# The second mixture's first steps taken batch by batch, with batch 0's operands made during the first mixture

## The chip, the cores and the metric

The kernel runs on one core of a Trainium2 chip: TensorE (PE, matrix products), VectorE (DVE), ScalarE (ACT), GpSimd (POOL) and SyncE (SP, which here only issues loads and stores). The metric is the device time of one execution in microseconds; less is better. A profiled execution gives a trace of every engine.

## The reference, cut to what matters

An attention with a local and a global window makes x (2 batches of 768 rows, 512 columns), then come two mixtures. The second is a layer norm, a product up to 2048 features, a relu, a product down, and a sum with its input:

```python
def _moe_ref(x, mu_k, mu_r, w_k, w_v, w_r):
    x_prev = np.concatenate([np.zeros((B, 1, D)), x[:, :-1, :]], axis=1)
    xk = mu_k * x + (1.0 - mu_k) * x_prev
    xr = mu_r * x + (1.0 - mu_r) * x_prev
    k = np.maximum(xk @ w_k, 0.0)
    v = k * k @ w_v
    r = 1.0 / (1.0 + np.exp(-(xr @ w_r)))
    return r * v

def _moe2_ref(x, g_ln, w_ch1, w_ch2):
    mu = np.mean(x, axis=-1, keepdims=True)
    var = np.mean((x - mu) ** 2, axis=-1, keepdims=True)
    xn = (x - mu) / np.sqrt(var + 1e-06) * g_ln
    ch = np.maximum(xn @ w_ch1, 0.0) @ w_ch2
    return x + ch
```

## The kernel before

Every operand of a product is split into a high and a low part, and a product of two operands is three products: high by high, low by high, high by low. A high part is a rounded copy (ScalarE); a low part is the operand less its high part (VectorE or GpSimd).

The first mixture works on six groups of 256 rows, `g` = 0 to 5; groups 0 to 2 are batch 0, 3 to 5 batch 1. For each group `plan_k` makes xk (`plan_mix`) and the product with `w_k` (L745), squares the relu (L754, L755) and splits it (L756, L760); `plan_r` does the gate (L709, tanh in L714); `plan_v` does the product with `w_v` (L786 to L788, three matmuls of 512 columns for each of 8 feature chunks and 2 row blocks) and, with the gate, writes x1 (L800). x1 of a group stays on the chip to the end and takes up the result.

The second mixture takes each batch of 768 rows as two halves of 384, interleaved by blocks of 128 rows, and does the product up by a scheme of seven products in place of eight (P1 to P7 in `plan_up`, L1029, six matmuls of 384 columns each), so it needs sums of blocks of the normalised rows and sums of blocks of the weights. `plan_norm(s, i, ...)` prepares block `i` of batch `s`: statistics (L819, L820, VectorE), root (L823, L824, GpSimd), normalised block `ln` (L832, VectorE), four transposes on TensorE into bank 7 (L828, called a turn here), copies (ScalarE), and, in line 834, sums and low parts. Of each two blocks, the even one gives the parts `b0h`/`b0l` (batch 0) or `b1h`/`yy` (batch 1), the odd one `b0r` or `m`/`u`, and both together eight sums in `h` that are split into `t0h`/`t0l` or `t1h`/`t1l`.

A step is one pair of feature chunks (`q` = 0 to 7, 256 features by the scheme's two halves) for one batch `s`. Before, step `k` is `q, s = divmod(k, 2)`: batch 0 and batch 1 in turn. `plan_up(k)` makes the seven products, adds them up out of the banks (L1037, VectorE), applies the relu and the high part (ScalarE) and the low part `h` (L1048). `plan_down(k)` multiplies with `w_ch2` (L1122 to L1124) and adds to x1 (L1128, L1138). `plan_w1` and `plan_w2` load and convert the weights of a pair (64-bit words: L590 or L588, L592 to L595), scale them (L973), make the four sums (L982 to L985) and split (L601, L605). The pair's first weights lie in `s0` or `s1`, by the parity of `q`.

The order is set by a planner, `Plan`: each operation names engines with an assumed duration, the cells it reads and writes, the rooms (buffers) it needs and a due time. `play` always takes the operation that can start first by the planner's own clock, and among equals the one due first. So an engine's order follows from these numbers; on the chip each engine then executes its instructions in that order. `self.mixed` and `self.free` are operations behind which others must stand: the last product of `plan_k` for the last group, and the last x1 of group 1.

Of the kernel before, what the change touches and what calls it, by code (L numbers as in the profile page):

```python
# [8 lines left out]
F32 = mybir.dt.float32  # L9
F32R = mybir.dt.float32r  # L10
# [6 lines left out]
P = 128  # L17
# [197 lines left out]
class Fast:  # L215
# [467 lines left out]

    def plan_r(self, g, due):

        nc, p = self.nc, self.plan
        if g < EG:
            z = Part([self.H0, self.token("xr", 1)], lambda t, _: t[:, 0:2].rearrange("p a b n -> p a (b n)"))
        else:
            z = self.room("t0h", 1, [P, 2, 1024], F32R)  # L690
        rooms = [z]
        put = lambda: tuple(z.tile[:, i].rearrange("p (c t) -> p c t", c=4) for i in range(2))
        self.plan_mix(g, 1, rooms, put, "xr", due)
        if g < 2:
            if g == 0:
                self.e01 = self.room("b0r", 1, [P, 4, 512])
            e = [(self.e01, lambda tb=tb: self.e01.tile[:, 2 * g + tb, :]) for tb in range(2)]
        else:
            zs = [self.room("g" if g % 2 else "e", 2, [P, 512]) for _ in range(2)]
            e = [(z, lambda z=z: z.tile) for z in zs]  # L700
        self.e[g] = e
# [62 lines left out]
    def plan_v(self, g, due):  # L764
# [7 lines left out]
        def make():  # L772
            x = self.x1[g] = self.t([P, 4 * (GT + 1)], "xg", bufs=6)
            return x

        x1 = Room("xg", 6, make, True)
        parts = [(tb, f, f + 4) for tb in range(2) for f in (0, 4)]
# [26 lines left out]
    def plan_norm(self, s, i, due, low_due):  # L804
# [8 lines left out]
        up = [self.mixed, self.x_op] if late else [self.mixed]  # L813
        o = slice(j * P, (j + 1) * P)
# [15 lines left out]
        p.op({"DVE": 850}, stats, [("x1", g, tb)], [N], [st], due, behind=[self.free])  # L830
        p.op({"POOL": 400}, root, [], [N], [st], due)
        p.op({"DVE": 550}, lambda e: nc.vector.tensor_scalar(y.tile, x(), st.tile[:, 6:7], st.tile[:, 0:1], ALU.subtract, ALU.mult), [], [N], [st, y], due + 1)  # L832
        p.op({"PE": 436}, turn, [], [N], [y, b], due + 2)
        sub = lambda e, z, u, v: (nc.vector if e == "DVE" else nc.gpsimd).tensor_tensor(z, u, v, ALU.subtract)
        if i % 2 == 0:
            hi, lo = (lambda z=z: z.tile[:, 0 : 4 * TS].rearrange("p (c t) -> p c t", c=4)[:, :, o] for z in X[0:2])
            p.op({"ACT": 590}, lambda e: self.copy(e, F(), b.tile), [N], [("F", j)], [b, prep], due + 3)
            p.op({"ACT": 590}, lambda e: self.copy(e, hi(), chunks(b.tile)), [N], [("B", s, i, 0)], [b, X[0]], due + 3)
            p.op({"POOL": 1440}, lambda e: sub(e, lo(), chunks(F()), hi().bitcast(F32)), [("F", j), ("B", s, i, 0)], [("B", s, i, 1)], [prep, *X[0:2]], low_due, behind=up)
            return  # L840
# [14 lines left out]
        else:  # L855
            p.op({"ACT": 400}, lambda e: self.copy(e, hi(), pair(y.tile[:, 256:512])), [N], [("B", s, i, 0)], [y, X[2]], due + 3)
            p.op({"POOL": 700}, lambda e: sub(e, lo(), pair(y.tile[:, 256:512]), hi().bitcast(F32)), [N, ("B", s, i, 0)], [("B", s, i, 1)], [y, *X[2:4]], due + 4)
        p.op({"DVE": 350} if s and i == 5 else {"POOL": 700}, lambda e: sub(e, T(2), T(1), F()[:, 0:256]), [Tt[1], ("F", j)], [Tt[2]], [prep], due + 4)
        p.op({"DVE": 350} if s and i == 5 else {"POOL": 700}, lambda e: sub(e, T(3), F()[:, 256:512], T(1)), [Tt[1], ("F", j)], [Tt[3]], [prep], due + 4)
        eight = lambda: prep.tile[:, 1536:2560].rearrange("p (k t) -> p k t", k=8)  # L860
        p.op({"ACT": 1050}, lambda e: self.copy(e, th(), eight()), Tt, [("T", s, i, 0)], [prep, X[4]], due + 5)
        p.op({"DVE": 1250} if s else {"POOL": 2500}, lambda e: sub(e, tl(), eight(), th().bitcast(F32)), [*Tt, ("T", s, i, 0)], [("T", s, i, 1)], [prep, *X[4:6]], due + 5)

    def first(self, last):
# [12 lines left out]
        with self.tc.manual_schedule(engines=ORDERED):  # L877
# [29 lines left out]
            self.plan_k(1, at[1], at[1] - 8)  # L907
            self.plan_v(0, at[1] + 12)
            for g in range(1, NG):
# [7 lines left out]
                if EG <= g + 1 < NG:  # L917
                    self.plan_r(g + 1, at[g + 1] - 12)
# [4 lines left out]
    def plan_second(self, start):  # L923
# [39 lines left out]
    def plan_w1(self, q, c, due, behind=()):  # L963
# [35 lines left out]
    def plan_up(self, k, due):  # L999

        nc, p = self.nc, self.plan
        q, s = divmod(k, 2)
# [6 lines left out]
        u3, order = 21, self.ORDER  # L1009
# [78 lines left out]
    FIRST = {"P1": -6.0, "P6": -5.7, "P7": -5.4, "P2": 0.0, "P4": 1.1, "P5": 2.2, "P3": 3.3}  # L1088
    ORDER = {"P1": 0.0, "P6": 1.1, "P5": 5.0, "P7": 6.1, "P2": 10.0, "P4": 11.1, "P3": 15.0}

    def plan_down(self, k, due):

        nc, p = self.nc, self.plan
        q, s = divmod(k, 2)
# [4 lines left out]
        for m in range(3):  # L1099
# [5 lines left out]
            elif k == 0 and m == 1:  # L1105
                rooms = [self.bank_room(i) for i in (3, 6)]
# [5 lines left out]
            d = due + (3 * m if lone else 2.2 + 4.9 * m if k else m - 6)  # L1112
# [256 lines left out]
```

## Time and profile before

| | |
|---|---|
| three runs, median (lowest to highest) | 563.97 us (563.05 to 565.64) |
| the profiled execution | 562.92 us |
| its span, first to last instruction | 561.1 us |
| mean granted clock of TensorE | 0.984 of full speed |
| TensorE matmuls busy | 528.3 us, 94% of the span |
| VectorE busy | 403.2 us, 72% |
| GpSimd busy | 305.0 us, 54% |
| ScalarE busy | 288.4 us, 51% |

Busy time is the time in which an engine has an instruction at work; the granted clock says how fast TensorE could run then. Matmuls overlap, so the distance from one start to the next is the price of one, not its own duration. A row of the timeline gives the start, the duration, the engine, the line, the tiles, and in brackets how long the engine stood idle before and what ended that. Batch 0's first turn is at 244.96 us, the last product of the first mixture ends at about 296.6 us, and the second mixture's first product is at 281.94 us.

### The profile page before, as it was taken

Reading aid. Unit: us, or ns where it says so; the run is one execution under the profiler, and the core shown is the slowest. Engines: PE = TensorE matmul, PEld = TensorE weight load, DVE = VectorE, ACT = ScalarE, POOL = GpSimd, SP = SyncE. Lnnn points to the kernel's source line nnn. Section 1 sums busy time; section 2 is a strip of 40 time slices with the busy share of each in tenths; the row PEclk is TensorE's granted clock in tenths of the full one; section 3 lists DMA queues with packets and bytes.
Section 4 is the critical chain, followed back from the end, with each engine's and each line's share of the span. In section 5 each row is a group of like instructions: output and inputs, shape, how many; then the busy total and the mean of one; then the engine's idle time right before and its main releaser. Section 6 shows DMA issues by size and latency. Waiting matters only on the chain.

```text
span 561.1 us, 8802 instructions
## 1 busy us (share of the span) xinstructions
PE 528.3 (94%) x3178; PEld 455.9 (81%) x3178; DVE 403.2 (72%) x766; ACT 288.4 (51%) x639; POOL 305.0 (54%) x365
## 2 busy tenths in 40 slices
PE   5879899999999999999797899999999999999995
PEld 4657677878799888888686798888998889888983
DVE  4987998776787535346979888767697767868463
ACT  2878877768453213245535365464555536464320
POOL 3266775565633121109777579586495738686200
PEclk9999999999999999999979899999999999999998
DMA  8899765512210000001210131313031311311024
GB/s 167 193 226 204 190 187 131 136 39 77 76 39 1 2 1 0 1 1 37 77 37 1 37 114 37 113 38 114 0 114 38 91 61 39 114 37 39 0 77 155
DMA packets 59456, 42.64 MB, mean 76 GB/s; under 512 B 49036, under 2 KB 49292, under 8 KB 59404
## 3 DMA queue, kind: packets, MB, share of 16 engines
q1 hardware_dynamic: 58796, 41.33, 28.1%
q8 instruction: 27, 0.44, 0.3%
q10 hardware_dynamic: 576, 0.66, 0.3%
q14 instruction: 25, 0.20, 0.1%
q0 software_dynamic: 32, 0.00, 0.0%
HBM read 38.84 MB, written 3.15 MB: 75 GB/s over the span
## 4 chain that ended last, share of the span: by engine, by line


## 5 line engine op out<-in xcount | busy, mean ns | idle before, releaser
L1128 DVE TENSOR_TENSOR xg<-b,xg 128x1024 f32<-128x1024 f32 x44 | 53.7, 1221 | 36.9 <-PE b L1124 36.4
L664 POOL TENSOR_SCALAR rt<-xg,vec 128x256 f32<-128x256 f32 x48 | 30.0, 638 | 41.0 <-DVE m L760 19.0
L595 DVE SCALAR_TENSOR_TENSOR cv<-cv,stage 128x512 int32<-128x512 int32 x50 | 46.2, 925 | 7.9 <-ACT cv L337 4.1
L1048 POOL TENSOR_TENSOR h<-rt,h 128x384 fp32r<-128x384 f32 x28 | 37.3, 1334 | 19.1 <-ACT h L337 19.1
L594 DVE SCALAR_TENSOR_TENSOR stage<-stage 128x512 int32<-128x512 int32 x50 | 47.1, 945 | 0.5
L501 ACT ACTIVATE t0l<-t0l,mn 128x232 f32<-128x232 f32 (+1 forms) x96 | 44.5, 467 | 4.4 <-DVE mn L495 4.2
L495 DVE CUSTOM_DVE_ANT_0 t0l<-b,ln 128x232 f32<-128x232 f32 (+1 forms) x96 | 32.0, 374 | 10.8 <-PE b L484 10.8
L605 POOL TENSOR_TENSOR s<-cv,s 128x384 fp32r<-128x384 f32 (+1 forms) x24 | 29.9, 1244 | 11.6 <-ACT s L601 11.6
L593 DVE TENSOR_SCALAR stage<-stage 128x512 int32<-128x512 int32 x50 | 33.7, 675 | 2.7 <-DMA stage<-in_moe_w_v_dram 1.6
L1048 POOL TENSOR_TENSOR h<-e,h 128x384 fp32r<-128x384 f32 x14 | 15.3, 1093 | 36.6 <-ACT h L337 36.6
L745 PE MATMUL b<-b0l,t1l 128*128 128x256 f32 x144 | 32.3, 283 | 0.0
L669 DVE SCALAR_TENSOR_TENSOR rt<-xg,vec,rt 128x256 f32<-128x256 f32 x48 | 29.7, 667 | 1.7 <-POOL rt L664 1.7
L1044 ACT ACTIVATE e<-e 128x384 f32<-128x384 f32 x16 | 8.4, 524 | 43.3 <-DVE e L1037 43.3
L1044 ACT ACTIVATE rt<-rt 128x384 f32<-128x384 f32 x32 | 16.7, 521 | 27.1 <-DVE rt L1037 27.1
L519 PE MATMUL b<-ident,t0l 128*116 128x128 f32 (+1 forms) x176 | 28.8, 280 | 1.3 <-ACT t0l L501 1.3
L534 PE MATMUL b<-yy,h 116*64 116x128 f32 (+1 forms) x352 | 24.5, 279 | 4.4 <-ACT yy L337 4.2
L1029 PE MATMUL b<-t0h,s 128*128 128x384 f32 x128 | 27.9, 339 | 0.0
L1029 PE MATMUL b<-t1h,s 128*128 128x384 f32 x128 | 27.7, 338 | 0.0
L534 PEld LDWEIGHTS b<-yy,h 116*64 116x64 f32 (+1 forms) x352 | 18.8, 136 | 10.3 <-ACT yy L337 7.8
L709 PE MATMUL b<-s,h 128*128 128x512 f32 x96 | 26.3, 410 | 0.1
L337 ACT ACTIVATE yy<-b 116x1024 f32<-116x1024 f32 (+1 forms) x24 | 22.8, 950 | 6.7 <-PE b L519 6.5
L484 PE MATMUL b<-b0h,b0l 64*128 64x232 f32 (+1 forms) x192 | 24.5, 368 | 1.6 <-ACT b0h L337 1.6
(300 smaller groups left out, 1666.1 us busy)
## 6 DMA issues: line engine op xcount, KB each, us to landing
stage<-in_moe_w_ch_dram SPq DMA_DIRECT2D x32, 512.0 KB
stage<-in_moe_w_k_dram SPq DMA_DIRECT2D x8, 512.0 KB
stage<-in_moe_w_v_dram SPq DMA_DIRECT2D x8, 512.0 KB
h<-in_v_dram SPq DMA_DIRECT2D x10, 192.0 KB
b0l<-in_q_dram SPq DMA_DIRECT2D x7, 256.0 KB
out_dram<-xg SPq DMA_DIRECT2D x3, 512.0 KB
stage<-in_moe_w_r_dram SPq DMA_DIRECT2D x2, 512.0 KB
b0h<-in_q_dram SPq DMA_DIRECT2D x4, 256.0 KB
```

Source lines behind the costliest of these rows:

```text
L495: nc.vector.tensor_tensor_reduce(tp.tile[:, k, 0:w], S(k), bias, slope(h), 3.0e38, ALU.add, ALU.min, mn.tile[:, k : k + 1])
L501: nc.scalar.activation(t, t, AF.Exp, bias=mn.tile[:, k : k + 1], scale=-1.0, accum_out=sm.tile[:, h : h + 1])
L534: nc.tensor.matmul(o, self.V[n].tile[0:w, c, h, :], y.tile[0:w, c, k * P : (k + 1) * P], start=c == 0, stop=c == m - 1)
L593: p.op({"DVE": 500}, lambda e: nc.vector.tensor_scalar(low(), low(), 29, None, ALU.logical_shift_right), [R], [(R, 1)], [raw], due - 2, be ...
L594: p.op({"DVE": 760}, lambda e: nc.vector.scalar_tensor_tensor(low(), high(), -(1 << 31), low(), ALU.bitwise_and, ALU.bitwise_or), [R, (R, ...
L595: p.op({"DVE": 760}, lambda e: nc.vector.scalar_tensor_tensor(y(), y(), 3, low(), ALU.logical_shift_left, ALU.bitwise_or), [(R, 2)], [C], ...
L605: (nc.vector if e == "DVE" else nc.gpsimd).tensor_tensor(lo, x(), hi.bitcast(F32), ALU.subtract)
L664: nc.gpsimd.tensor_scalar(y.tile[:, u], z, v, 0.0, ALU.mult, ALU.add)
L745: nc.tensor.matmul(o, l, r, start=s == 0, stop=s == 11)
L1029: nc.tensor.matmul(acc(x), lhs(i, c, n), rhs(r, j, c), start=y == 0, stop=y == 5)
L1048: lambda e: (nc.vector if e == "DVE" else nc.gpsimd).tensor_tensor(o(1), V(y), o(0).bitcast(F32), ALU.subtract),
L1128: p.op({"DVE": 1250}, lambda e, x=x, z=rooms[0]: nc.vector.tensor_tensor(x(), z.tile.rearrange("p a n -> p (a n)"), x(), ALU.add), cells, ...
```

## The change

1. The steps go in the order `(0,0), (1,0), (0,1), (1,1)` for the first four (a pair of feature chunks and a batch), then as before. Due times of steps, weights and norms follow; the second pair's weights are planned ahead of the steps and no longer behind a step's products. The first step's and the second step's products have orders of their own (`FIRST`, `SECOND`).
2. Batch 0's blocks are prepared from the third group of the first mixture on. Their low parts and sums, on GpSimd before, are on VectorE; batch 0's first operands (`b0h`, `b0l`) are written only behind the last gate product (`self.gone`). For batch 1, the last block's sums move from VectorE to GpSimd.
3. To make room, the gate of the fifth and sixth group uses the buffer `b0h` in place of `t0h`, and is made for both behind group 1's `plan_k` (`self.k1`); the fifth group's gate is kept in the tile that will be its x1.
4. The second pair's weight sums and low parts may go to VectorE; the buffers of `w_ch2` turn in another order. The planner's durations for the norm are larger.

```diff
@@ plan_r @@
-            z = self.room("t0h", 1, [P, 2, 1024], F32R)
+            z = self.room("b0h", 1, [P, 2, 1024], F32R)
-        self.plan_mix(g, 1, rooms, put, "xr", due)
+        self.plan_mix(g, 1, rooms, put, "xr", due, [self.k1] if g >= EG else ())
+            if g == EG:
+                home = self.x1_room(g)
+                e = [(home, lambda tb=tb: home.tile[:, tb * 512 : (tb + 1) * 512]) for tb in range(2)]
@@ plan_v @@
-        parts = [(tb, f, f + 4) for tb in range(2) for f in (0, 4)]
+        parts = [(tb, f, f + 4) for f in (0, 4) for tb in range(2)]
@@ plan_norm @@
+        early = s == 0
-        p.op({"DVE": 850}, stats, [("x1", g, tb)], [N], [st], due, behind=[self.free])
-        p.op({"POOL": 400}, root, [], [N], [st], due)
+        p.op({"DVE": 950}, stats, [("x1", g, tb)], [N], [st], due, behind=[self.free])
+        p.op({"POOL": 950}, root, [], [N], [st], due)
-            p.op({"POOL": 1440}, lambda e: sub(e, lo(), chunks(F()), hi().bitcast(F32)), [("F", j), ("B", s, i, 0)], [("B", s, i, 1)], [prep, *X[0:2]], low_due, behind=up)
+            if early:
+                p.op({"ACT": 630}, lambda e: self.copy(e, hi(), chunks(F())), [("F", j)], [("B", s, i, 0)], [prep, X[0]], low_due - 1, behind=[self.gone])
+            p.op({"DVE": 715} if early else {"POOL": 1440}, lambda e: sub(e, lo(), chunks(F()), hi().bitcast(F32)), [("F", j), ("B", s, i, 0)], [("B", s, i, 1)], [prep, *X[0:2]], low_due, behind=up)
-        p.op({"DVE": 350} if s and i == 5 else {"POOL": 700}, lambda e: sub(e, T(2), T(1), F()[:, 0:256]), [Tt[1], ("F", j)], [Tt[2]], [prep], due + 4)
+        p.op({"DVE": 350} if early else {"POOL": 700}, lambda e: sub(e, T(2), T(1), F()[:, 0:256]), [Tt[1], ("F", j)], [Tt[2]], [prep], due + 4)
-        p.op({"DVE": 1250} if s else {"POOL": 2500}, lambda e: sub(e, tl(), eight(), th().bitcast(F32)), [*Tt, ("T", s, i, 0)], [("T", s, i, 1)], [prep, *X[4:6]], due + 5)
+        p.op({"DVE": 1400}, lambda e: sub(e, tl(), eight(), th().bitcast(F32)), [*Tt, ("T", s, i, 0)], [("T", s, i, 1)], [prep, *X[4:6]], due + 5)
@@ first @@
-                    self.plan_r(g + 1, at[g + 1] - 12)
+                    self.plan_r(g + 1, at[EG] - 12 + 12 * (g + 1 - EG))
+                    self.gone = self.r_op
@@ plan_second @@
-        at = [T0 + UP * k for k in range(2 * PAIRS + 1)]
+        at = [T0, T0 + 4, *(T0 + 22 + UP * k for k in range(2 * PAIRS - 1))]
+        self.steps = [(0, 0), (1, 0), (0, 1), (1, 1), *((q, s) for q in range(2, PAIRS) for s in range(2))]
-            self.plan_norm(0, i, start - 30 + 4 * i, start - 8 + i)
+            self.plan_norm(0, i, start - 66 + 8 * i, start - 20 + i)
+        for c in range(2):
+            self.plan_w1(1, c, at[0] - 12 + 2 * c)
-            if k % 2 and k < 2 * PAIRS - 1:
+            if k % 2 and 1 < k < 2 * PAIRS - 1:
@@ plan_w1 @@
-        p.op({"POOL": 1800}, sums, [C], [(key, "S")], [raw, cv], due)
+        p.op({"DVE": 920} if q == 1 else {"POOL": 1800}, sums, [C], [(key, "S")], [raw, cv], due)
@@ plan_w2 @@
-        parts = self.w2rooms[(f + 2) % 4]
+        parts = self.w2rooms[(3, 2, 0, 1)[f % 4]]
@@ plan_up, plan_down @@
-        q, s = divmod(k, 2)
+        q, s = self.steps[k]
-    FIRST = {"P1": -6.0, "P6": -5.7, "P7": -5.4, "P2": 0.0, "P4": 1.1, "P5": 2.2, "P3": 3.3}
+    FIRST = {"P1": -6.0, "P6": -5.7, "P7": -5.4, "P2": -7.0, "P4": -6.9, "P5": -6.8, "P3": -6.7}
+    SECOND = {"P1": 0.0, "P6": 0.1, "P5": 0.2, "P7": 11.0, "P2": 12.1, "P4": 13.2, "P3": 14.3}
```

Lines after 683 have other numbers in the changed kernel: L828 becomes L836, L832 L840, L834 L842, L800 L807, L1029 L1047, L1122 to L1124 L1141 to L1143, L982 to L985 L1000 to L1003, L755 L766, L760 L771, L823 and L824 L831 and L832.

**TensorE, from the first step's last products on.** `b0...` are parts of batch 0, `b1h` and `yy` of batch 1, `s_...` the pair's first weights. Before:

```order
L1029 MATMUL b_419_3195<-t0h_2812,s_354_2763 128x384 x4
L1029 MATMUL b_419_3195<-t0l_2832,s_354_2763 128x384 x2
L828 MATMUL b_421_3207<-ident,ln_3193 128x128 x4
L1029 MATMUL b_424_3216<-b0r_2767,s_354_2763 128x384 x6
L1122 MATMUL b_425_3228<-b0r_2767,h_422_3212 128x512
L1123 MATMUL b_425_3228<-s_354_2763,h_422_3212 128x512
L1124 MATMUL b_425_3228<-b0r_2767,h_422_3212 128x512
L1122 MATMUL b_426_3235<-b0r_2767,h_422_3212 128x512
L1123 MATMUL b_426_3235<-s_354_2763,h_422_3212 128x512
L1124 MATMUL b_426_3235<-b0r_2767,h_422_3212 128x512
L1029 MATMUL b_427_3248<-b1h_3038,s_354_2763 128x384 x4
L1029 MATMUL b_427_3248<-yy_3166,s_354_2763 128x384 x2
```

Now:

```order
L1047 MATMUL b_418_3205<-t0h_2468,s_349_2668 128x384 x4
L1047 MATMUL b_418_3205<-t0l_2481,s_349_2668 128x384 x2
L1047 MATMUL b_421_3219<-b0r_2450,s_349_2668 128x384 x6
L1141 MATMUL b_425_3241<-b0h_2685,h_423_3229 128x512
L1142 MATMUL b_425_3241<-b0l_2975,h_423_3229 128x512
L1143 MATMUL b_425_3241<-b0h_2685,h_423_3229 128x512
L1141 MATMUL b_426_3247<-b0h_2685,h_423_3229 128x512
L1142 MATMUL b_426_3247<-b0l_2975,h_423_3229 128x512
L1143 MATMUL b_426_3247<-b0h_2685,h_423_3229 128x512
L1047 MATMUL b_427_3253<-b0h_2685,s_395_3074 128x384 x4
L1047 MATMUL b_427_3253<-b0l_2975,s_395_3074 128x384 x2
```

The second step's first product was batch 1's with the first pair's weights and is now batch 0's with the second pair's.

**VectorE, around the normalised block of batch 1's first turn** (`xg_2677` before and `xg_2789` now are x1 of the fourth group; `ln_3016` and `ln_2898` the block). Before, at the end of the fifth group:

```order
L594 SCALAR_TENSOR_TENSOR stage_2932<-stage_2932 128x512
L800 SCALAR_TENSOR_TENSOR xg_2993<-e_2461,b_365_2836 128x512
L760 TENSOR_TENSOR yy_1937<-rt_2973,yy_1937 128x512
L755 SCALAR_TENSOR_TENSOR rt_3010<-b_374_2895,rt_3010 128x512
L832 TENSOR_SCALAR ln_3016<-xg_2677,st_2892 128x512
L800 SCALAR_TENSOR_TENSOR xg_2993<-e_2505,b_365_2836 128x512
```

Now:

```order
L593 TENSOR_SCALAR stage_2704<-stage_2704 128x512
L827 BN_STATS st_2863<-xg_2789 128x6
L828 BN_AGGR st_2863<-st_2863 128x2
L842 TENSOR_TENSOR t0l_2481<-h_309_2330,t0h_2468 128x8x128
L594 SCALAR_TENSOR_TENSOR stage_2704<-stage_2704 128x512
L840 TENSOR_SCALAR ln_2898<-xg_2789,st_2863 128x512
L595 SCALAR_TENSOR_TENSOR cv_2757<-cv_2757,stage_2704 128x512
```

The block stood between the two instructions that take up the fifth group's product (L800), and now stands 18 rows ahead of them, with batch 0's low part (`t0l`) on this engine.

**GpSimd, from the first pair's weight splits (`s_...`) on.** Before:

```order
L605 TENSOR_TENSOR s_354_2763<-cv_1942,s_354_2763 128x384
L605 TENSOR_TENSOR s_354_2763<-stage_1888,s_354_2763 128x512
L834 TENSOR_TENSOR t0l_2832<-h_346_2703,t0h_2812 128x8x128
L834 TENSOR_TENSOR b0l_2948<-h_346_2703,b0h_2716 128x4x128 x2
L834 TENSOR_TENSOR b0r_2767<-ln_2888,b0r_2767 128x2x128
L834 TENSOR_TENSOR h_346_2703<-h_346_2703 128x256 x2
L823 TENSOR_SCALAR st_2892<-st_2892 128x1
L824 TENSOR_TENSOR st_2892<-st_2892,mhalf_119 128x1
```

Now:

```order
L605 TENSOR_TENSOR s_349_2668<-cv_1942,s_349_2668 128x384
L605 TENSOR_TENSOR s_349_2668<-stage_1888,s_349_2668 128x512
L664 TENSOR_SCALAR rt_2736<-xg_1549,vec_121 128x256 x2
L664 TENSOR_SCALAR rt_2754<-xg_1549,vec_121 128x256 x2
L341 TENSOR_SCALAR cv_2787<-stage_2740 128x512
L831 TENSOR_SCALAR st_2863<-st_2863 128x1
L832 TENSOR_TENSOR st_2863<-st_2863,mhalf_119 128x1
```

Batch 0's low parts and sums are gone from this queue, and the sixth group's xk (L664) stands behind the splits.

## Rows read from the trace of the kernel before

**Rows 1.** The page: granted clock of TensorE in 40 slices, in tenths.

```profile
PEclk9999999999999999999979899999999999999998
```

**Rows 2.** Windows: stretch, length, busy of PE, PEld, DVE, ACT, POOL, clock, DMA.

```profile
198.18:324.64 126.46, 117.22 (x638) 102.00 (x637) 82.57 (x129) 52.11 (x95) 63.07 (x76) 0.95 0.07 22
...
324.64:400.00 75.36, 75.16 (x374) 67.56 (x374) 58.52 (x80) 37.51 (x76) 52.03 (x53) 1.00 0.25 77
```

**Rows 3.** What TensorE waited for, 240 to 324.6 us: total, times, longest.

```profile
PE b L828 <- DVE ln L832: 4.9, 2, 3.6
PE b L1124 <- DVE h L1048: 2.3, 1, 2.3
PE b L1029 <- POOL yy L834: 2.0, 1, 2.0
```

**Rows 4.** Timeline of TensorE around the seam: start, duration, engine, line, tiles.

```profile
281.20 1.09 PE L828 MATMUL b<-ident,ln 128*128 128x128 f32 x4 [3.58 <-DVE ln L832]
...
284.01 0.63 PE L786 MATMUL b<-h,yy 128*128 128x512 f32 x1
284.43 0.63 PE L787 MATMUL b<-h,yy 128*128 128x512 f32 x1
...
286.57 0.44 PE L786 MATMUL b<-h,yy 128*128 128x512 f32 x1
...
288.01 0.60 PE L828 MATMUL b<-ident,ln 128*128 128x128 f32 x4
288.36 0.95 PE L1029 MATMUL b<-t0h,s 128*128 128x384 f32 x4
...
310.00 0.79 PE L1124 MATMUL b<-b0h,h 128*128 128x512 f32 x1 [2.31 <-DVE h L1048]
...
313.99 0.40 PE L1124 MATMUL b<-b0r,h 128*128 128x512 f32 x1
314.23 0.40 PE L1122 MATMUL b<-b0h,h 128*128 128x512 f32 x1
...
319.44 0.85 PE L1029 MATMUL b<-t1h,s 128*128 128x384 f32 x4
...
320.47 0.85 PE L1029 MATMUL b<-t1h,s 128*128 128x384 f32 x4
```

**Rows 5.** Timeline of VectorE, 267 to 282 us.

```profile
267.32 0.68 DVE L819 BATCH_NORM_STATS2 st<-xg 128x6 f32<-128x512 f32 x1
...
268.13 1.81 DVE L593 TENSOR_SCALAR stage<-stage 128x512 int32<-128x512 int32 x1
...
274.93 0.42 DVE L593 TENSOR_SCALAR stage<-stage 128x512 int32<-128x512 int32 x1
...
281.57 2.27 DVE L760 TENSOR_TENSOR yy<-rt,yy 128x512 fp32r<-128x512 f32 x1
```

**Rows 6.** Timeline of GpSimd in the same stretch.

```profile
266.81 2.85 POOL L834 TENSOR_TENSOR t0l<-h,t0h 128x1024 fp32r<-128x1024 f32 x1
...
280.73 2.55 POOL L834 TENSOR_TENSOR t0l<-h,t0h 128x1024 fp32r<-128x1024 f32 x1
```

**Rows 7.** Windows of 8 us, 264 to 312 us: two of six, and their sum.

```profile
264.00:272.00 8.00, 8.00 (x51) 7.14 (x52) 7.75 (x10) 3.04 (x5) 8.00 (x6) 1.00 0.23 68
...
296.00:304.00 8.00, 8.00 (x49) 7.47 (x48) 7.19 (x14) 6.25 (x14) 6.63 (x8) 1.00 0.01 2
...
sum 48.00, PE 40.08 PEld 34.10 DVE 42.91 ACT 23.99 POOL 36.21; mean PE 6.68 PEld 5.68 DVE 7.15 ACT 4.00 POOL 6.03
```

**Rows 8.** Groups of GpSimd's instructions, 244 to 324 us: busy us, mean ns.

```profile
L834 POOL TENSOR_TENSOR t0l<-h,t0h 128x1024 fp32r<-128x1024 f32 x3 | 8.0, 2659 | 0.0
...
L983 POOL TENSOR_TENSOR stage<-stage,cv 128x128 f32<-128x128 f32 x2 | 0.9, 460 | 0.2
```

**Rows 9.** The page: two groups of GpSimd's instructions of the whole execution.

```profile
L1048 POOL TENSOR_TENSOR h<-rt,h 128x384 fp32r<-128x384 f32 x28 | 37.3, 1334 | 19.1 <-ACT h L337 19.1
...
L605 POOL TENSOR_TENSOR s<-cv,s 128x384 fp32r<-128x384 f32 (+1 forms) x24 | 29.9, 1244 | 11.6 <-ACT s L601 11.6
```

More of the change, by code (lines that the diff above doesn't have):

```diff
@@ L682, in plan_mix, with x1_room, make @@
             p.op(LATE_LOW if g >= (EG if m else 1) else LOW, low, [Y, (cell, g, s, 0)], [(cell, g, s, 1)], [y] + rooms, due)
+    def x1_room(self, g):
+        def make():
+            x = self.x1[g] = self.t([P, 4 * (GT + 1)], "xg", bufs=6)
+            return x
+        return self.x1rooms.setdefault(g, Room("xg", 6, make, True))
     def plan_r(self, g, due):
@@ L698, in plan_r @@
         else:
-            zs = [self.room("g" if g % 2 else "e", 2, [P, 512]) for _ in range(2)]
+            zs = [self.room("g" if g == 3 else "e", 2, [P, 512]) for _ in range(2)]
             e = [(z, lambda z=z: z.tile) for z in zs]
+            if g == EG:
+                home = self.x1_room(g)
+                e = [(home, lambda tb=tb: home.tile[:, tb * 512 : (tb + 1) * 512]) for tb in range(2)]
         self.e[g] = e
@@ L770, in plan_v @@
         acc = lambda tb: b[0].tile if last and not tb else b[1].tile[:, tb]
[L772 to L776, printed above, removed]
-        parts = [(tb, f, f + 4) for tb in range(2) for f in (0, 4)]
+        x1 = self.x1_room(g)
+        parts = [(tb, f, f + 4) for f in (0, 4) for tb in range(2)]
         if not last:
@@ L907, in first @@
             self.plan_k(1, at[1], at[1] - 8)
+            self.k1 = self.k_op
             self.plan_v(0, at[1] + 12)
@@ L947, in plan_second @@
         for c in range(2):
-            self.plan_w1(0, c, at[0] - 18 + 5 * c)
+            self.plan_w1(0, c, at[0] - 32 + 5 * c)
         for c in range(2):
-            self.plan_w2(c, at[1] - 18 + 5 * c)
+            self.plan_w2(c, at[0] - 18 + 5 * c)
+        for c in range(2):
+            self.plan_w1(1, c, at[0] - 12 + 2 * c)
+        for c in range(2):
+            self.plan_w2(2 + c, at[0] + 12 + 5 * c)
         self.up, self.step = [], []
@@ L954, in plan_second @@
             self.plan_down(k, at[k + 1])
-            if k % 2 and k < 2 * PAIRS - 1:
+            if k % 2 and 1 < k < 2 * PAIRS - 1:
                 q = (k + 1) // 2
-                gates = [self.step[k - 1]["P2" if k > 1 else "P3"], self.step[k]["P1"], self.step[k]["P2"]]
+                gates = [self.step[k - 1]["P2"], self.step[k]["P1"], self.step[k]["P2"]]
                 self.plan_w1(q, 0, at[k] - 4, gates[0:1])
@@ L1008, in plan_up @@
         v = {x: self.room(t, 2, [P, 512]) for x, t in ((11, "rt"), (22, "e"), (21, "g"), (12, "rt"))}
-        u3, order = 21, self.ORDER
+        u3, order = 21, self.ORDER if k > 1 else self.SECOND
         if k == 0:
@@ L1093, in plan_down @@
         nc, p = self.nc, self.plan
-        q, s = divmod(k, 2)
+        q, s = self.steps[k]
         h = self.h
@@ L1105, in plan_down @@
             elif k == 0 and m == 1:
-                rooms = [self.bank_room(i) for i in (3, 6)]
+                rooms = [self.bank_room(i) for i in (6, 0)]
                 acc = [lambda z=z: z.tile for z in rooms]
@@ L1111, in plan_down @@
                 acc = [lambda z=z, i=i: z.tile[:, i] for i in range(2)]
-            d = due + (3 * m if lone else 2.2 + 4.9 * m if k else m - 6)
+            d = due + (3 * m if lone else 2.2 + 4.9 * m if k else m + 0.5)
             cells = []
@@ L1146, in run @@
     def run(self, last):
-        self.x1, self.e = {}, {}
+        self.x1, self.e, self.x1rooms = {}, {}, {}
         self.first(last)
```

13 lines of the change are left out of this document (7 added, 6 removed).

## The prediction

> **What bounds the kernel now.** I read the clock and busy rows first, then the windows, then TensorE's waits, then its timeline around them. TensorE is the bound: after 324.64 us it is busy 75.16 of 75.36 us at the full clock [rows 2]. Only around the seam between the two mixtures, and in the last slice, does the granted clock fall [rows 1]. So the seam is where time can be won.
>
> I take the stretch from 198.18 us, where TensorE's order first differs, to 324.64 us, where the third step of the second mixture begins; it lasts 126.46 us, and 5% of the clock is missing in it [rows 2]. TensorE waits there four times: twice for a normalised block from VectorE before a turn (4.9 us together, 3.6 the longest, so 1.3 and 3.6), 2.3 us for a low part of the hidden values, and 2.0 us for a low part that GpSimd makes [rows 3]. That is 9.2 us. After the two long gaps it runs at half speed: matmuls of 512 columns start 0.42 us apart at 284.01 us and 0.24 us apart at 313.99 us [rows 4], the levels of 1.2 and 2.4 GHz. The slow stretches are 281.20 to 286.57 us and 310.00 to 313.99 us [rows 4], 5.4 and 4.0 us; half of each is lost, 4.7 us. **What the seam can give back is 9.2 + 4.7 = 13.9 us.**
>
> **The work on TensorE** changes in order only: the order of the changed kernel holds the same products up to the first product of the third step. With no wait it gets there 13.9 us earlier. The four waits, one by one. The turns of batch 0 now stand among products of the fourth, fifth and sixth group, so the 1.3 us wait (a turn of batch 0) goes. The 3.6 us wait was a turn of batch 1 after four triples (one triple: three matmuls of the first mixture's second product) of the last group; its VectorE instruction now stands far ahead of the turn. The 2.0 us wait was for batch 1's low parts in the second step; that step now takes batch 0. The 2.3 us wait was for the first step's hidden values, with VectorE busy on batch 1's parts; now two more products, two more triples and a turn lie between.
>
> **VectorE takes work from GpSimd.** Per batch 0 that is three low parts of 512 columns, three of 256, six sums of 256 and three low parts of 1024. GpSimd's price for the last is 2659 ns each, 8.0 us [rows 8]; on VectorE an undisturbed 512-column instruction takes 0.68 us [rows 5], and at that rate per column (an estimate) the fifteen take about 10 us, where GpSimd, at the rate of its 2659 ns for 1024 columns, spends some 19. For the second feature pair's weights the sums of 128 columns move too: on GpSimd 460 ns each [rows 8]. VectorE shows no such instruction; between 0 and GpSimd's 0.46 us I take 0.25, half-way, since it has half the columns of a 256-column one. Eight of them and four low parts make about 4.5 us. These lie beside TensorE's products as long as VectorE keeps up, so I cost them at nothing there and price the lag instead.
>
> **Does VectorE keep up?** The tight part begins at the end of the fifth group's second product (call it E). From E to the second product of the third step TensorE has 28 triples (0.70 each, three starts of 0.235), six turns (0.35, 288.01 to 288.36 us) and 15 products (1.03, 319.44 to 320.47 us) [rows 4]: 19.6 + 2.1 + 15.5 = 37.2 us. VectorE has 65 instructions up to the low part which that product needs. At the pace of 296 to 304 us (7.19 us for 14, 0.51 each) they take 33 us; at the mean of the six windows from 264 to 312 us (42.91 us for 68, 0.63) they take 41 [rows 7]. So the lag is between nothing and 3.8 us. I take 2.0 us: less GpSimd work than in those windows, but the instructions are not evenly spread. The tightest place: from E to the third turn of batch 1 VectorE has 27 instructions, 13.8 us at 0.51 each, and TensorE 48 matmuls, two turns and two products, 14.0 us.
>
> **Moved behind other things.** SP's order of loads is unchanged, and nothing is added to its queue. The sixth group's first operands are now made behind four weight splits on GpSimd; their last VectorE instruction now stands behind one that waits for the end of the fourth group. Eight full-rate matmuls come before TensorE needs it; I cost that at 0 to 0.5 us, inside the 2.0. The third pair's weights now have to be remade between the third and the fifth step, since two pairs run side by side; TensorE has 15 triples and 7 products there, 17.7 us, and GpSimd needs eight sums (0.46), four splits (1.244) and four low parts of hidden values (1.334) [rows 8, 9], 14.0 us. So it costs nothing, and 1 us for each us by which that chain is over 3.7 us longer.
>
> **The sum.** The profiled execution took 562.92 us with a span of 561.1. 562.92 − 13.9 + 2.0 = 551.0 us. The median of the three runs before is 563.97, 1.05 above the profiled execution; on that footing the forecast is 552.0 us.
>
> **Rivals.**
> 1. *GpSimd blocks VectorE.* At 268.13 us a VectorE instruction took 1.81 us which at 274.93 took 0.42; it ended 0.28 us after the GpSimd instruction that had begun at 266.81 and took 2.85. At 281.57 one took 2.27 us, until 0.56 after GpSimd's of 280.73 (2.55 us). The statistics at 267.32, with one operand, kept their 0.68 [rows 5, 6]. So a two-operand instruction in on-chip memory waits for the whole of GpSimd's. By the Trainium skill (SBUF — State Buffer, "Who interferes with whom") the two share one port pair and hold it exclusively, whoever issues first; the trace agrees. Work put on VectorE is then only safe while GpSimd is quiet. From E to the fourth turn of batch 1 GpSimd still has six such instructions (two sums, a conversion, three low parts); at 1.244 us each [rows 9] 7.5 us. If VectorE meets half of them late, it falls 3.8 us behind on top of an order without slack, and one half-speed stretch returns (2.7): 549.0 + 6.5 = 555.5 us, 556.5 on the median's footing; if it meets all of them, 560.2. Against it: some 19 us of GpSimd's work are gone.
> 2. *The wait moves and stays.* VectorE at 0.70 us each needs 45.5 us from E: 8.3 lost, and both half-speed stretches (4.7): 562.0 us, 563.1 on the median's footing.
> 3. *Slower: VectorE becomes the bound of the seam.* At the pace of 264 to 272 us (7.75 us for 10, 0.775 [rows 7]) it needs 50.4 us, 13.2 more than TensorE, and the clock costs 4.7: 17.9 lost against 13.9 won, 566.9 us, 568.0 on the median's footing. It decides from 0.76 us per instruction. For it: VectorE has more to do. Against: that pace was seen with GpSimd busy for 8.00 of 8 us [rows 7].
> 4. *Nothing is lost*: 549.0, 550.1 on the median's footing.
>
> That the change does not do what it says is no rival: the order shows the steps by batch and batch 0's parts on VectorE.
>
> **Chances.** Forecast (0.5 to 4 us lost, 550.5 to 554) 0.60; rival 1 (554 to 559) 0.20; rival 4, 0.07; rival 2 (559 to 566) 0.08; rival 3, 0.05. The range 549.5 to 559.0 holds the forecast, rival 1 and part of rival 4. A measurement of this kernel can tell about 0.5% (2.8 us) from no change. Faster by more: the forecast, rivals 1 and 4 and little else, 0.88; within it: most of rival 2, 0.07; slower: rival 3, 0.05.
>
> **What would show it.** Right: in the changed profile the clock row stays full around the seam, no wait of TensorE for a turn is over 1.3 us, and the first product on batch 1's first operand (the third step) begins near 312.7 us (324.64 − 13.9 + 2.0). Rival 1: a turn or a low part waits for VectorE, and the VectorE instruction ahead ends just after one of GpSimd's. Rivals 2 and 3: two waits over 2 us with the clock low behind them. I am wrong too if TensorE waits at the fifth step for GpSimd's weights, or in the stretch before E.

## The result and the profile after

The changed kernel takes 555.29 us (median of four, 554.46 to 556.07), the kernel before, run beside it, 564.18: a ratio of 0.9841, 95% interval 0.9813 to 0.9869. The profiled execution took 556.07 us with a span of 554.2.

The clock row of the page, to set beside [rows 1]:

```profile
PEclk9699999999999999999999999999999999999999
```

The dips around the seam are gone. There is one near the start now. Windows of the changed kernel (columns as in [rows 2]): 15 to 20 us, then from the point where TensorE's order first differs (198.18 us before, 200.80 now) to the third step's first product, and from there to the last product:

```profile
15.00:20.00 5.00, 4.86 (x26) 3.37 (x26) 4.10 (x23) 3.14 (x11) 0.83 (x2) 0.50 1.12 246
200.80:313.19 112.39, 111.94 (x639) 98.51 (x638) 84.81 (x155) 52.36 (x95) 38.35 (x51) 1.00 0.10 32
313.19:546.57 233.38, 229.97 (x1129) 203.74 (x1128) 169.06 (x228) 109.73 (x219) 137.32 (x142) 1.00 0.20 64
```

The same stretch of the kernel before, from its third step to its last product:

```profile
324.64:553.88 229.24, 228.64 (x1128) 204.22 (x1128) 169.71 (x228) 109.51 (x217) 139.97 (x144) 1.00 0.22 69
```

So the 126.46 us of [rows 2] are 112.39: **the seam gives back 14.07 us**. But the rest of the second mixture, in which only the third step is another than before, takes 233.38 instead of 229.24: **4.14 us are lost after the third step begins**. The start (2.62 us later at the seam, with TensorE at 1.2 GHz from 15 to 20 us) belongs to this execution: another one of the same kernel (c0_after below) has the full clock there and reaches the seam at 197.13 us. The sum against the profile before: 562.92 + 2.62 − 14.07 + 4.14 + 0.4 (behind the last product) = 556.0 us.

What TensorE waited for, from 200.8 to 313.2 us (first row, in place of [rows 3]) and from 313 to 547 us (the others):

```profile
PE b L756 <- DVE rt L766: 0.5, 1, 0.5
...
PE b L1047 <- DVE e L1055: 1.5, 2, 0.9
PE b L1141 <- DVE xg L1147: 1.5, 4, 0.6
PE b L1143 <- POOL h L1066: 0.4, 1, 0.4
```

Of the four waits of the seam none is left. One new wait of 0.5 us stands in it, for a squared relu of the first mixture (L766). Behind it there are 3.4 us of waits; the kernel before had 0.6 there:

```profile
PE b L1122 <- DVE xg L1128: 0.6, 3, 0.2
```

So 2.8 of the 4.14 us are waiting; by the remaining 1.3 us TensorE is counted busy longer (229.97 against 228.64). A wait costs more than the idle time beside it, as the first of these shows below, but no row accounts for all of the 1.3. The four longest waits on TensorE's timeline, behind the third step's first product:

```profile
313.19 0.85 PE L1047 MATMUL b<-b1h,s 128*128 128x384 f32 x4
...
315.04 0.93 PE L1047 MATMUL b<-t1h,s 128*128 128x384 f32 x4 [0.65 <-DVE e L1055]
...
337.87 0.50 PE L1141 MATMUL b<-b0h,h 128*128 128x512 f32 x1 [0.58 <-DVE xg L1147]
...
353.58 0.49 PE L1143 MATMUL b<-b1h,h 128*128 128x512 f32 x1 [0.37 <-POOL h L1066]
...
356.30 0.98 PE L1047 MATMUL b<-b1h,s 128*128 128x384 f32 x4 [0.87 <-DVE e L1055]
```

VectorE's timeline shows what stood ahead of two of them:

```profile
276.29 0.69 DVE L807 SCALAR_TENSOR_TENSOR xg<-xg,b 128x512 f32<-128x512 f32 x1 [0.44 <-PE b L795]
...
313.04 1.39 DVE L842 TENSOR_TENSOR t1l<-h,t1h 128x1024 fp32r<-128x1024 f32 x1 [0.38 <-ACT t1h L337]
314.35 0.55 DVE L1055 TENSOR_TENSOR e<-b,g 128x384 f32<-128x384 f32 x1
...
333.82 1.17 DVE L593 TENSOR_SCALAR stage<-stage 128x512 int32<-128x512 int32 x1
335.02 1.67 DVE L594 SCALAR_TENSOR_TENSOR stage<-stage 128x512 int32<-128x512 int32 x1
336.61 1.21 DVE L1147 TENSOR_TENSOR xg<-b,xg 128x1024 f32<-128x1024 f32 x1
```

The third step's second product starts 1.85 us after its first, where a product takes 1.03 [rows 4], so 0.8 us went there, of which 0.65 are idle: the sum that frees the bank stood behind batch 1's last low part. At 337.87 it stood behind two word instructions (L593 and L594; with L595 they put the 64-bit weights together) that took 1.17 and 1.67 us. Meanwhile GpSimd split the third pair's weights:

```profile
333.68 1.02 POOL L605 TENSOR_TENSOR s<-cv,s 128x384 fp32r<-128x384 f32 x1
334.66 1.47 POOL L605 TENSOR_TENSOR s<-stage,s 128x512 fp32r<-128x512 f32 x1
```

The other two belong to a burst: ScalarE writes the fourth step's hidden values (`h`) only at 350.75 us, although the fourth step's last product up ended at 337.3 us:

```profile
350.75 0.53 ACT L337 ACTIVATE h<-e 128x384 fp32r<-128x384 f32 x1 [0.82 <-PE b L1143]
```

It waited for the last product down of the third step: both steps belong to batch 1 and share one buffer, since `h` has one for each batch.

### The profile page after: what moved, and what is told of

Its sections match the earlier page's. It is cut to its first block, busy times and chain, and to the rows that moved or that the text cites. A ratio compares the mean times of both kernels' runs of the same rounds, so it can differ in the third digit from the quotient of the medians.

```text
span 554.2 us, 8779 instructions
## 1 busy us (share of the span) xinstructions
PE 528.0 (95%) x3178; PEld 454.2 (82%) x3178; DVE 403.8 (73%) x791; ACT 288.2 (52%) x641; POOL 278.6 (50%) x338
## 4 chain that ended last, share of the span: by engine, by line
## 5 line engine op out<-in xcount | busy, mean ns | idle before, releaser
L1147 DVE TENSOR_TENSOR xg<-b,xg 128x1024 f32<-128x1024 f32 x44 | 53.6, 1219 | 39.5 <-PE b L1143 39.3
L595 DVE SCALAR_TENSOR_TENSOR cv<-cv,stage 128x512 int32<-128x512 int32 x50 | 43.9, 879 | 8.9 <-ACT cv L337 5.0
L594 DVE SCALAR_TENSOR_TENSOR stage<-stage 128x512 int32<-128x512 int32 x50 | 46.8, 938 | 0.6
L1066 POOL TENSOR_TENSOR h<-rt,h 128x384 fp32r<-128x384 f32 x28 | 35.9, 1281 | 15.3 <-ACT h L337 15.3
L664 POOL TENSOR_SCALAR rt<-xg,vec 128x256 f32<-128x256 f32 x48 | 29.9, 639 | 15.6 <-DVE m L771 4.3
L605 POOL TENSOR_TENSOR s<-cv,s 128x384 fp32r<-128x384 f32 (+1 forms) x22 | 26.8, 1217 | 19.0 <-ACT s L601 19.0
L831 POOL TENSOR_SCALAR st<-st 128x1 f32<-128x1 f32 x12 | 4.5, 375 | 60.2 <-DVE st L828 60.0
L593 DVE TENSOR_SCALAR stage<-stage 128x512 int32<-128x512 int32 x50 | 30.9, 620 | 2.8 <-DMA stage<-in_moe_w_v_dram 1.6
L519 PE MATMUL b<-ident,t0l 128*116 128x128 f32 (+1 forms) x176 | 30.1, 287 | 1.5 <-ACT t0l L501 1.5
L1047 PE MATMUL b<-t1h,s 128*128 128x384 f32 x128 | 27.8, 339 | 0.6 <-DVE e L1055 0.6
L1047 PE MATMUL b<-t0h,s 128*128 128x384 f32 x128 | 27.9, 339 | 0.0
L519 PEld LDWEIGHTS b<-ident,t0l 128*116 128x116 f32 (+1 forms) x176 | 20.1, 139 | 8.5 <-issue 3.8
```

The source lines that it names most:

```text
L519: nc.tensor.transpose(b.tile[0:w, c, k * P : (k + 1) * P], tp.tile[:, k, c * w : (c + 1) * w], self.ident)
L593: p.op({"DVE": 500}, lambda e: nc.vector.tensor_scalar(low(), low(), 29, None, ALU.logical_shift_right), [R], [(R, 1)], [raw], due - 2, be ...
L594: p.op({"DVE": 760}, lambda e: nc.vector.scalar_tensor_tensor(low(), high(), -(1 << 31), low(), ALU.bitwise_and, ALU.bitwise_or), [R, (R, ...
L595: p.op({"DVE": 760}, lambda e: nc.vector.scalar_tensor_tensor(y(), y(), 3, low(), ALU.logical_shift_left, ALU.bitwise_or), [(R, 2)], [C], ...
L664: nc.gpsimd.tensor_scalar(y.tile[:, u], z, v, 0.0, ALU.mult, ALU.add)
L1047: nc.tensor.matmul(acc(x), lhs(i, c, n), rhs(r, j, c), start=y == 0, stop=y == 5)
```

## The experiments

The theory at this point: the early parts won the seam, and the new step order costs the 4.14 us, by the shared buffer and by VectorE's queue. The rivals: the step order or the engine wins the seam; GpSimd holding VectorE is all of the loss. Times are medians. Ratios, with their 95% intervals, are to the kernel before on the same chip; its medians lie between 563.07 and 564.42 us there, so kernels of different groups are compared by ratio or by trace.

### What won the seam

**a1_steps_undone**: changed kernel, old step order with its due times and with the second pair's weights and the buffers of `w_ch2` that go with it. From the diff:

```diff
-        self.steps = [(0, 0), (1, 0), (0, 1), (1, 1), *((q, s) for q in range(2, PAIRS) for s in range(2))]
+        self.steps = [divmod(k, 2) for k in range(2 * PAIRS)]
```

> The changed kernel with the steps of the second mixture in the old order again (batch 0 and batch 1 in turn, with the old due times of steps and second-pair weights); batch 0's early parts on VectorE stay. Theory A (the early parts remove the waits for batch 0's turns and the first half-speed stretch, the step order removes the other half of the seam's loss and costs 4.5 us after the third step begins): of the 13.9 us of the seam 1.3 + 3.6 + 2.7 = 7.6 stay won, the waits of 2.0 and 2.3 us and their 2.0 us of half speed come back, and the 4.5 us are not lost: 564.2 - 7.6 = 556.6 us, with waits for batch 1's parts between the first and the second step. Rival B (the early parts alone win the whole seam): 564.2 - 13.9 = 550.3 us. Rival C (without the new step order nothing is won, since batch 1's turns wait as before): 562 us or more.

It takes 556.06 us, ratio 0.9872 (0.9839 to 0.9906), where A gave 556.6. The three longest sums of TensorE's waits from 196 us on:

```profile
PE b L1137 <- DVE xg L1143: 2.0, 5, 1.0
PE b L1139 <- DVE h L1062: 1.2, 2, 1.0
PE b L836 <- DVE ln L840: 1.0, 1, 1.0
```

The waits for hidden values and for a turn (the second and third row) are back, but short (A had 2.0 and 2.3 and a slow stretch). The seam and what follows, cut as above:

```profile
197.88:314.42 116.54, 112.83 (x638) 98.27 (x637) 84.87 (x142) 52.27 (x95) 46.89 (x62) 1.00 0.07 23
314.42:545.84 231.42, 229.43 (x1129) 204.02 (x1128) 172.44 (x228) 111.02 (x220) 139.19 (x144) 1.00 0.22 68
```

So 9.92 of the 14.07 us come without the new step order; the 0.003 between this ratio and the changed kernel's is inside the intervals. A expected no loss behind the seam with the old order, and there it was wrong: 231.42 us are 2.18 more than before. All five waits of the first row lie there, and the longest, 1.03 us at 332.04, is again for a sum behind a word instruction of 1.05 us:

```profile
329.80 1.05 DVE L593 TENSOR_SCALAR stage<-stage 128x512 int32<-128x512 int32 x1
330.77 1.21 DVE L1143 TENSOR_TENSOR xg<-b,xg 128x1024 f32<-128x1024 f32 x1
```

So waits in VectorE's queue come without the new step order, too, and the order is not shown to be all of the 4.14 us.

**a3_steps_alone**: kernel before, new step order and weights planned ahead, nothing else.

> The kernel before with the new step order alone (and the second pair's weights planned ahead); batch 0's parts are made late and on GpSimd as before. Theory A (the order removes the waits for batch 1's parts, the turns of batch 0 and 1 still come late, and 4.5 us are lost after the third step begins): 564.2 - 2.0 - 2.3 - 2.0 + 4.5 = 562.4 us, with the two waits for turns still there. Rival B (the order alone wins the seam and loses the 4.5 us): 564.2 - 13.9 + 4.5 = 554.8 us. Rival C (the second step now waits for the second pair's weights, behind GpSimd's late parts): slower than 564.2 us.

It takes 565.83 us, ratio 1.0053 (1.0032 to 1.0074): slower, as C had it, but not by its mechanism. TensorE waited for turns, longer than before, and not for weights:

```profile
PE b L828 <- DVE ln L832: 5.9, 3, 4.8
PE b L1034 <- DVE rt L1042: 2.2, 1, 2.2
```

Behind the seam the order brings a loss of its own, 3.26 us against the 229.24 before, where A had 4.5:

```profile
323.27:555.77 232.50, 229.76 (x1129) 203.85 (x1128) 168.10 (x227) 109.36 (x219) 137.19 (x141) 1.00 0.20 63
```

**a2_parts_on_pool**: changed kernel, batch 0's parts on GpSimd.

```diff
-        p.op({"DVE": 1400}, lambda e: sub(e, tl(), ...
+        p.op({"DVE": 1400} if s else {"POOL": 2500}, lambda e: sub(e, tl(), ...
```

(so for the other low parts and sums)

> The changed kernel with batch 0's low parts and sums on GpSimd again, at the new early times. Theory A (what counts is that they are made early; GpSimd is busy only 15.7 of 51.8 us from 198 to 250 us and 20.5 of 60 us from 250 to 310, so some 19 us more fit): within 1.5 us of the changed kernel, 554 to 557 us, with no wait over 1 us in the seam. Rival B (the engine counts: GpSimd's longer instructions hold VectorE's, at 1.2 to 1.9 us over the undisturbed time each, and TensorE waits again for a turn or a low part): 558 us or more, and VectorE's 512-column instructions at over 1.2 us in the trace from 250 to 310 us.

It takes 553.74 us, ratio 0.9843 (0.9811 to 0.9875), the changed kernel's. Windows from 250 to 310 us, this kernel and the changed one (GpSimd's is the fifth busy time):

```profile
250.00:310.00 60.00, 59.55 (x336) 53.04 (x335) 53.00 (x93) 29.97 (x56) 32.95 (x36) 1.00 0.14 45
```

```profile
250.00:310.00 60.00, 59.55 (x333) 52.23 (x332) 54.30 (x100) 29.29 (x56) 20.51 (x26) 1.00 0.12 36
```

GpSimd is busy 12.4 us longer, TensorE the same 59.55. The engine is not what won.

**c4_late_due**: changed kernel, batch 0's old due times.

```diff
-            self.plan_norm(0, i, start - 66 + 8 * i, start - 20 + i)
+            self.plan_norm(0, i, start - 30 + 4 * i, start - 8 + i)
```

> The changed kernel with the old due times of batch 0's blocks alone (from 30 us ahead of the seam, 4 us apart, where the changed kernel has 66 and 8); the step order, the engines and the buffers stay as changed. Theory A (what won the 13.9 us of the seam is that batch 0's blocks are made early): its turns come late among the products again, waits of TensorE for turns of 3 us or more and a stretch at 1.2 GHz come back, ratio to the kernel before 0.99 or more (558 us and up). Rival B (the work on VectorE and the new buffers suffice, the times follow by themselves): within 0.003 of the changed kernel's ratio of 0.984.

It takes 569.08 us, ratio 1.0093 (1.0068 to 1.0118): with this one line undone, all of the gain is lost, and more. One turn waits 6.2 us, and the clock falls:

```profile
PE b L836 <- DVE ln L840: 6.2, 1, 6.2
```

```profile
290.00:310.00 20.00, 14.23 (x63) 13.33 (x64) 16.00 (x35) 10.68 (x22) 10.34 (x13) 0.74 0.19 54
```

A had the long wait at a turn of batch 0. This one, at 294.76 us, is the ninth turn and so one of batch 1: batch 0's last low part of 1024 columns now stands on VectorE at 279.50 us, among batch 1's blocks, where the changed kernel has it at 259.91. The run shows that the early due times are needed; alone, without the buffers that make room for them, they were not run.

### What was lost behind it

**b2_hidden**: changed kernel, hidden values by the step's number from the third step on.

```diff
-        h = self.h = self.room(f"h{s}", 1, [P, 2, 2, 2, TS], F32R)
+        h = self.h = self.room(f"h{s if k < 2 else (k + 1) % 2}", 1, [P, 2, 2, 2, TS], F32R)
```

> The changed kernel with the hidden values of the fourth step in the other buffer: from the third step on the two buffers are used in turn, where the changed kernel has one buffer for each batch, so that the fourth step (batch 1 again) can write its hidden values only when the products down of the third step have read theirs. Theory A (this shared buffer makes the burst at 350 us, with the waits of 0.37 us for GpSimd's low part and 0.87 us for VectorE and what follows them, 2.1 us over the pace of products at 352.8 to 356.4 us): those waits go, 555.3 - 2.1 = 553.2 us; the waits at 315.0 and 337.9 us stay (0.65 and 0.58). Rival B (the waits come from GpSimd holding VectorE while the third and fourth pairs' weights are made, wherever the hidden values lie): waits of the same sum at other places, 555.3 us within 0.7.

It takes 552.63 us, ratio 0.9815 (0.9785 to 0.9845); the interval holds the changed kernel's ratio too, so the trace has to tell. From the third step to the last product:

```profile
310.84:542.78 231.94, 229.12 (x1129) 203.88 (x1128) 171.38 (x228) 110.48 (x219) 136.93 (x142) 1.00 0.20 64
```

These are 231.94 us against 233.38 (and 233.97 in c0_after). The burst is gone, but a wait of 1.20 us for the sum L1147 came in its place at 361 us: 1.4 us won (2.0 against c0_after), not the 2.1 at the burst alone.

**c0_after**, **c1_quiet** and **c2_words_longer** ran together on one chip.

> The changed kernel again, unaltered, beside the three that follow, to set them against it on one chip, and to see whether the slow stretch of the clock at its start (12.8 to 23 us, 2.6 us) belongs to the kernel. Theory A (it belongs to an execution, not to the kernel: up to 198 us the two kernels have the same order): 0.984 of the kernel before, executions 2 to 3 us apart, some without that stretch. Rival B (it belongs to the changed kernel): the stretch is there again in the trace.

It takes 554.14 us (552.47 to 557.77), ratio 0.9843 (0.9815 to 0.9870). Its trace has the full clock at the start, the same seam (112.37) and a loss of 4.73 us behind it (233.97):

```profile
15.00:20.00 5.00, 4.31 (x39) 2.98 (x39) 4.66 (x25) 3.71 (x11) 2.10 (x3) 1.00 1.12 250
197.13:309.50 112.37, 111.91 (x639) 98.51 (x638) 84.84 (x155) 52.35 (x95) 39.17 (x51) 1.00 0.11 32
309.50:543.47 233.97, 230.21 (x1128) 203.73 (x1128) 169.92 (x228) 109.58 (x219) 136.50 (x142) 1.00 0.20 63
```

For c1_quiet, with `b2_hidden` as its base:

```diff
+            if q in (2, 3):
+                return
```

(ahead of GpSimd's four sums, and likewise ahead of its low parts: 16 sums and 8 low parts are left out, and stale weights are used)

> The kernel b2_hidden with GpSimd's work on the weights of the third and fourth pair left out (sixteen sums, eight low parts): the order of all other instructions is the same, and the stale weights are used. Theory A (the waits of 0.75 us at 334.6 us and 1.36 us at 359.9 us of b2_hidden come because VectorE's word instructions ahead of the sum that TensorE waits for are held by GpSimd's: 1.17 and 1.67 us where 0.42 and 0.69 are undisturbed): both go, 2.1 us, 0.996 of b2_hidden's time, with the word instructions at 0.42 to 0.70 us there. Rival B (VectorE's order alone makes them: the sum is queued behind word instructions that may well be undisturbed): each is still 0.4 us or more, and the time is within 0.8 us of b2_hidden's. The wait at 311.7 us (0.65 us for VectorE behind the last low part of batch 1) stays by both.

It takes 549.95 us, ratio 0.9764 (0.9745 to 0.9782). From the third step on it needs 229.90 us, 2.04 less than b2_hidden, as A had it. VectorE ahead of the sum L1147 for which TensorE waits at 335.5 us, in b2_hidden:

```profile
331.49 1.15 DVE L593 TENSOR_SCALAR stage<-stage 128x512 int32<-128x512 int32 x1
332.67 1.67 DVE L594 SCALAR_TENSOR_TENSOR stage<-stage 128x512 int32<-128x512 int32 x1
```

and in c1_quiet:

```profile
330.61 0.42 DVE L593 TENSOR_SCALAR stage<-stage 128x512 int32<-128x512 int32 x1
331.07 0.69 DVE L594 SCALAR_TENSOR_TENSOR stage<-stage 128x512 int32<-128x512 int32 x1
```

So GpSimd's work held them, 1.7 us together. By the Trainium skill (SBUF — State Buffer, "Who interferes with whom") such instructions of the two engines take turns on a shared port pair; the trace agrees. The wait at 361 us had another path: in b2_hidden ScalarE stood still for GpSimd's sum, and VectorE's last word instruction then waited 2.47 us for ScalarE:

```profile
357.52 0.64 ACT L601 ACTIVATE s<-stage 128x512 fp32r<-128x512 f32 x1 [1.04 <-POOL stage L1003]
```

```profile
359.21 1.05 DVE L595 SCALAR_TENSOR_TENSOR cv<-cv,stage 128x512 int32<-128x512 int32 x1 [2.47 <-ACT cv L337]
```

For c2_words_longer, b2_hidden with other planner durations alone (0.8, 1.4 and 1.3 us for the three word instructions, from the third pair on):

```diff
-        p.op({"DVE": 760}, lambda e: nc.vector.scalar_tensor_tensor(low(), high(), ...
+        p.op({"DVE": 1400 if self.late else 760}, lambda e: nc.vector.scalar_tensor_tensor(low(), high(), ...
```

> The kernel b2_hidden with larger durations in the planner for VectorE's word instructions of the third and later pairs (0.8, 1.4 and 1.3 us for 0.5, 0.76 and 0.76): no instruction is added or left out; VectorE's sums for TensorE (L1147, L1055) come to stand ahead of them. Theory A (the waits after the third step's begin come from that queue): the waits for the sum L1147 at 334.6 and 359.9 us shrink below 0.4 us each, 1 to 2 us less than b2_hidden, 550.6 to 551.6 us where b2_hidden has 552.6. Rival B (the words themselves then come late, and TensorE waits for weights): the same or slower than b2_hidden, with a wait for a weight of the third pair or later.

It takes 549.78 us, ratio 0.9754 (0.9736 to 0.9772): **better than both kernels**, with all the work in it. From the third step on it is 2.8 us faster than b2_hidden, where A had 1 to 2, and as fast as the kernel before (229.24):

```profile
313.18:542.35 229.17, 228.11 (x1129) 204.12 (x1128) 169.49 (x228) 106.36 (x218) 136.10 (x143) 1.00 0.21 65
```

The way there is not quite A's. Ahead of the same sum (L1148 in this kernel) the same two word instructions still stand, now with other sums between them. They took 0.51 and 0.68 us, and the sum began as soon as TensorE let it:

```profile
334.02 0.51 DVE L593 TENSOR_SCALAR stage<-stage 128x512 int32<-128x512 int32 x1
...
335.38 0.68 DVE L594 SCALAR_TENSOR_TENSOR stage<-stage 128x512 int32<-128x512 int32 x1
336.30 1.22 DVE L1148 TENSOR_TENSOR xg<-b,xg 128x1024 f32<-128x1024 f32 x1 [0.24 <-PE b L1144]
```

GpSimd's work is all there. Its split beside L594 was the one that took long this time, 1.85 us, where the same took 1.30 at 364.05 us of b2_hidden:

```profile
335.38 1.85 POOL L605 TENSOR_TENSOR s<-stage,s 128x512 fp32r<-128x512 f32 x1
```

So another order of the same work costs TensorE nothing. Which of the instructions that the planner moved brings the 2.8 us is not shown.

**d1_words_alone**: the same durations in the changed kernel, with batch 1's shared buffer.

> The changed kernel with the larger planner durations of VectorE's word instructions alone, the hidden values of the fourth step in batch 1's buffer as changed. Theory A (the shared buffer and VectorE's queue each cost about half of the 4.1 us after the third step begins): the wait at 333.3 us for the sum L1147 shrinks, the burst at 349 to 353 us (low part 0.37, VectorE 0.87) stays: 1 to 2 us less than the changed kernel, 2 to 3 more than with both (ratio 0.980 to 0.983). Rival B (the queue is all of it): ratio as with both, 0.9754 within 0.002. Rival C (the buffer is all of it): ratio 0.984.

It takes 555.59 us, ratio 0.9826 (0.9802 to 0.9850). The ratio falls where A put it, but its interval holds the changed kernel's too, and the trace shows no gain: 233.63 us from the third step on, with the burst still there and a longer wait ahead of it.

```profile
353.36 0.47 PE L1142 MATMUL b<-b1h,h 128*128 128x512 f32 x1 [1.41 <-DVE xg L1148]
354.68 0.51 PE L1144 MATMUL b<-b1h,h 128*128 128x512 f32 x1 [0.61 <-POOL h L1067]
```

So the two causes do not add: against the changed kernel's 233.38 us the buffer alone gives 1.4 us, the durations alone nothing that shows, both 4.2.

**c3_hidden_pool**: b2_hidden with batch 0's parts on GpSimd.

> The kernel b2_hidden with batch 0's parts on GpSimd. If the engine of these parts does not matter (a2_parts_on_pool was within 1 us of the changed kernel's ratio), within 1 us of b2_hidden; if VectorE's load in the seam were what is left, 1 to 2 us faster.

It takes 553.09 us, ratio 0.9810 (0.9791 to 0.9830), b2_hidden's: once more the engine does not matter.

## Why the prediction was right or wrong

- **What the seam can give back** (13.9 us): right, 14.07. All four waits and both slow stretches went, and a new wait of 0.5 us is already taken off.
- **VectorE's lag** (between 0 and 3.8, taken as 2.0): too large. From 276.29 us (the 65 instructions begin) to 314.43 (the low part ends) VectorE took 38.14 us, 0.587 each, between the two paces of [rows 7]. TensorE lost 0.8 us, at the third step's second product.
- **GpSimd's relief**: the work moved at no cost, but it was not needed; a2_parts_on_pool gives it back for nothing. The gain needs the early due times (c4_late_due); 9.92 us of it come without the step order (a1_steps_undone). The fifteen instructions come to 9.2 and 17.9 us by the two rates that the prediction names, not to 10 and 19; neither is a term of its sum.
- **The third pair's weights** ("so it costs nothing"): the step that failed. The chain of sums and splits did end in time (its last split at 336.1 us, the fifth step's first product at 340.75), and I looked no further. Beside it VectorE's words took 1.17 and 1.67 us in place of 0.42 and 0.69, and the sum that TensorE needed stood behind them. That is rival 1's mechanism, behind the seam where I had it in the seam. Rival 1 had it for two-operand instructions alone, but its own first row (268.13 us, 1.81 for 0.42) is L593, which reads one operand.
- **The steps behind the third**: left out of the sum. Two successive steps of one batch share a buffer for hidden values; the diff's step list showed it, and I did not ask which buffers alternate by batch. With the two together 4.14 us went missing; the new order of the `w_ch2` buffers is no part of it, since c2_words_longer keeps it and loses nothing. Waits in VectorE's queue are not the new order's alone: a1_steps_undone, without it, loses 2.18 us there.
- **The sum**: 551.0 forecast for a profiled execution. With what was measured it is 562.92 − 14.07 + 4.14 = 553.0 (the lag of 0.8 is in the 4.14); c0_after's profiled execution took 552.63, and the one with the slow start 556.07. The median of 555.29 lies in the range, but in rival 1's part of it (554 to 559) and not in the forecast's own (550.5 to 554). That it lies there is partly luck: the 2.0 us set down for a lag that cost 0.8 cover a part of the 4.14 that the sum left out.
- **What would show it**: the first product on batch 1's first operand came at 313.19 us where I had 312.7, but with 2.62 us of late start in it; on equal footing 310.57.

Not settled: whether the new step order is worth its place once the buffer and the queue are mended. a1_steps_undone and the changed kernel differ by less than their intervals; by their traces the order wins 4.15 us in the seam and loses 1.96 to 2.55 behind it (233.38 and 233.97 against 231.42). The old order with the mended queue was not run.

## What to carry to other kernels

Before moving steps, list what alternates by the old order (buffers, banks, weight slots): what took turns by batch does so no longer when one batch comes twice in a row. A gain at a seam is to be followed to the end of the program, and an operand's due time comes first: undoing one line of due times cost more here (0.025 of the ratio) than undoing the engine (nothing) or the step order (0.003). Where a planner sets the order, durations that hold only beside an idle neighbour give a plan that the chip does not keep; longer ones for the instructions that another engine holds up cost nothing, and won 0.9% together with the buffer, alone nothing that shows.

## What the runs showed of the hardware

VectorE's single-operand word instruction (L593) was held by GpSimd as well as its two-operand ones: 1.15 and 1.17 us against 0.42. The hold goes either way: where GpSimd's split and VectorE's L594 both began at 335.38 us (c2_words_longer), L594 kept its 0.68 us and the split took 1.85 where 1.30 is the same split's time in b2_hidden. The clock at the start is a matter of the execution: with the same order up to 198 us, TensorE ran at 1.2 GHz from 15 to 20 us in one execution and at 2.4 GHz in another, and reached the seam at 200.80 and 197.13 us.
